# SiLU written back into its PSUM bank, and VectorE multiplying there, in a Strassen gate/up unit

## The chip, the cores and the metric

The kernel runs on one core of a Trainium2 chip. The metric is the device time of one execution in microseconds; the median of three runs of the kernel before is 1667.53 us. The engines are called as in the profile: PE (TensorE) does the matmuls and writes PSUM, ACT is ScalarE, DVE is VectorE, POOL is GpSimd, SP issues most of the DMAs.

## What is computed

One layer with two branches over a normalized input, sequence length 2048 and model width 576:

```python
xn = _layernorm(x, axis=-1)
s = _A_ref(xn, A_wqkv, A_w_phi, A_wo)        # linear attention, 32 heads of 18
g = _silu(_B_ref(xn, B_w_gate, B_w_up, B_w_down))
return x + s * g
```

The second branch is the one that matters here, a gated feed-forward network with a hidden width of 4608:

```python
def _B_ref(x, w_gate, w_up, w_down):
    g = _silu(x @ w_gate)
    u = x @ w_up
    return (g * u) @ w_down
```

Everything is float32. Matrix products run as three products of a rounded part and a remainder ("split"): a cast on ScalarE gives the rounded part, a subtraction on VectorE the remainder.

## The kernel before

The attention branch, the normalization and six of the 36 hidden tiles (128 hidden columns each, line 110, "early" tiles) come first and take about 541 us. The rest of the span is the feed-forward branch, and the change lies there.

The sequence is handled in two halves of 1024 rows (index i of the main loop, line 870). For each half, 30 hidden tiles are computed by `gate_up` (line 591), one call each, here called a unit; the six early tiles are fetched back from DRAM by `stored` (line 583). So there are 60 units in all. A unit forms the gate and the up product of 128 hidden columns with all 1024 rows. The gate and up weights beside each other and the two half blocks of rows make a 2x2 block product, which is done with seven block products in place of eight (Strassen's scheme with sums of blocks, Winograd's form). `product` (line 566) is one of them: seven matmuls of 512 columns into one PSUM bank.

A unit has four PSUM banks of 128x512 in view: x (`px`, two buffers, so that consecutive units alternate), y (`py`, one buffer) and w (`pw`, one buffer). The down part (`item`, line 785, and `tile_of`, line 685) has two buffers `pd` of two banks each. [...] In order of the program a unit does this:

- x gets product 0; ScalarE copies x to y (line 611); w gets product 4; y gets product 1 on top of the copy, and is then the gate product of the first row block;
- ScalarE applies SiLU to y and writes `h[0]`, an SBUF tile named `ha` (line 615);
- x goes on with products 5 and 2, and after each ScalarE copies it to an SBUF tile `s` (`snap`, line 596: s2 and s3);
- VectorE adds w to s3 (`add`, line 602; the add is line 604); x gets product 6 and is then the gate product of the second row block; SiLU writes `h[1]`, named `hb` (line 625), and VectorE multiplies it by s3 (line 626);
- w gets product 3, VectorE adds it to s2, and multiplies `h[0]` by s2 (line 630).

Between the products stand calls of `fill` (line 846). It emits matmuls of the down part from a queue: items that multiply finished h tiles, or sums of them, with rows of w_down, again by Strassen's scheme (`strassen`, line 730). The sums of h tiles and of w_down blocks are made on GpSimd (lines 753 to 779), then split (lines 58 and 59, the cast and the subtraction of `split`, used for h tiles `hh`, down weights `dw` and gate/up weights `w`). The result of an item is added to an accumulator in SBUF by VectorE (line 794; the accumulators are `acc`, `X` and `sx`). In the first half, the gate/up weights of the next tile are loaded and their sums made on GpSimd (lines 557 to 560) and split; they are also written to DRAM, and the second half reads them from there.

The program is written with a framework that tracks the tiles, sets the semaphores and lays out the instructions of each engine ahead of the run: each engine executes its queue in order, but that order is chosen by a planner from priorities (`tc.high_priority()`), the operands' modelled readiness and the buffers that are free. So it departs from the order of the program, as where the first product of the next unit runs ahead of the last product of this one. The last multiply of a unit is kept as an anchor (line 630): a few later groups of instructions are told to be issued behind it (`tc.issue_after`, lines 801 and 898).

Of the kernel before, what the change touches and what calls it, by code (L numbers as in the profile page):

```python
# [11 lines left out]
AF = mybir.ActivationFunctionType  # L12
# [34 lines left out]
def gated_hedgehog_kernel(ctx: ExitStack, tc, x, w_qk, w_v, w_phi, wo, w_gu, w_tail, w_down, ident_in, mask_in, out):  # L47
# [5 lines left out]
    nc = tc.nc  # L53
# [512 lines left out]
    def product(ps, w, m, b, first, last):  # L566
        mm = [(w[0][m][:, i], b[j]) for c in range(2) for i, j in ((c, c), (2 + c, c), (c, 3 + c))]
        mm += [(w[1][:, m], b[2][0:96])]
        for n, (l, r) in enumerate(mm):
            nc.tensor.matmul(ps, l, r, start=first and n == 0, stop=last and n == len(mm) - 1, skip_group_check=True)  # L570

    def short(name, bufs):
        return fq.tile([P, BT], F32, name=name, bufs=bufs)

    def h_tile():
        return [fp.tile([P, BT], F32, name=n, bufs=b) for n, b in (("ha", 7), ("hb", 6))]
# [6 lines left out]
    def stored(src, fill):  # L583
        h = h_tile()
        for r in range(2):
            nc.sync.dma_start(h[r], src[:, r * BT:(r + 1) * BT])
        for _ in range(4):
            fill()
        return h

    def gate_up(w, xo, fill, opening):
        A11, A12, A22, S2, S4, S3, S1 = xo
        xp, yp, wp = (fps.tile([P, BT], F32, name=n, bufs=b) for n, b in (("px", 2), ("py", 1), ("pw", 1)))
        h = h_tile()

        def snap(ps):
            t = short("s", 3)
            with tc.high_priority():
                nc.scalar.copy(t, ps)  # L599
            return t  # L600

        def add(ps, t):
            with tc.high_priority():
                nc.vector.tensor_add(t, ps, t)  # L604


        if opening:
            nc.tensor.matmul(yp, w[0][0][:, 0], A11[0], start=True, stop=True)
        product(xp, w, 0, A11, True, False)
        with tc.high_priority():  # L610
            nc.scalar.copy(yp, xp)  # L611
        product(wp, w, 4, S1, True, False)
        fill()
        product(yp, w, 1, A12, False, True)
        nc.scalar.activation(h[0], yp, AF.Silu)
        product(xp, w, 5, S2, False, False)
        s2 = snap(xp)
        fill()
        product(xp, w, 2, S3, False, False)
        s3 = snap(xp)  # L620
        add(wp, s3)
        fill()
        product(xp, w, 6, A22, False, True)
        with tc.high_priority():
            nc.scalar.activation(h[1], xp, AF.Silu)
        nc.vector.tensor_mul(h[1], h[1], s3)  # L626
        product(wp, w, 3, S4, False, True)
        add(wp, s2)
        with tc.high_priority():
            anchor.append(nc.vector.tensor_mul(h[0], h[0], s2))  # L630
        fill()
        return h

# [200 lines left out]
    queue, anchor, share = [], [], [2]  # L834
# [11 lines left out]
    def fill(lag=LAG):  # L846
        done = 0
        while queue and done < share[0] and (sum(c for q in queue for c, _ in q[2]) > lag or not queue[0][0]):
            look()
            c, item = queue[0][2].pop(0)  # L850
            item()
            done += c
            if not queue[0][2]:
                queue.pop(0)
# [15 lines left out]
    for i, n, f in units:  # L870
# [3 lines left out]
        if f >= EARLY:  # L874
# [3 lines left out]
            if todo and (i, f) != (0, NF - 1):  # L878
                ready.append(gate_up_weights(*todo.pop(0)))
        h = stored(h_dram[i, f], fill) if f < EARLY else gate_up(w, xo, fill, (i, f) == (0, EARLY))  # L880
        if n % 2 == 0:
            g = {"f": (f, units[units.index((i, n, f)) + 1][2]), "h": [h]}
# [58 lines left out]
```

## Time and profile before

| | |
|---|---|
| median of three runs | 1667.53 us (1667.0 to 1669.49) |
| span of the profiled execution | 1666.4 us |
| granted TensorE clock, mean | 0.997 |
| PE busy | 1621.8 us, 97% of the span |
| DVE busy | 1218.2 us, 73% |
| ACT busy | 718.3 us, 43% |
| POOL busy | 632.7 us, 38% |
| 60 units and the down part | from about 541 us to the end |

The profiled execution's time from first to last instruction is its span, 1.1 us below the median of the runs. PEld is TensorE's loading of weights, which overlaps the matmuls. In a row of groups or of the timeline stands the engine, the line of the kernel, the operation, the tile written and the tiles read (an arrow between them) and the shapes; a bracket at the end of a timeline row says how long the engine had been idle and whose result ended that. The waits view names the engine and line that waited, after the arrow the engine and line that it waited for, then the total in us, how many times, and the longest. The windows view gives, for a stretch of time, its length and the busy time and number of instructions of PE, PEld, DVE, ACT and POOL, then PE's granted clock, the DMA share and GB/s.

### The profile page before, as it was taken

What the parts mean: (1) busy time and instruction counts of PE and PEld (TensorE: products, weight loads), DVE (VectorE), ACT (ScalarE), POOL (GpSimd) and SP (SyncE); (2) the same over time, 40 slices, a digit from 0 to 9 for tenths busy, and PEclk for the clock granted to TensorE, in tenths of its full rate; (3) what the DMA queues carried; (4) which work ended last, traced back from release to release, by engine and by line L of the source; (5) the groups of instructions that cost most, each with busy time, mean ns of one, the idle gap of its engine ahead of it and who ended that gap; (6) DMA issues with size and microseconds to landing.
All of it is one profiled execution on the core that took longest, in us unless ns stands there. A gap on an engine that the chain in (4) does not pass through costs nothing.

```text
span 1666.4 us, 25130 instructions
## 1 busy us (share of the span) xinstructions
PE 1621.8 (97%) x9441; PEld 1437.4 (86%) x9441; DVE 1218.2 (73%) x1722; ACT 718.3 (43%) x1389; POOL 632.7 (38%) x660
## 2 busy tenths in 40 slices
PE   6999999999999999999999999999999999999998
PEld 5899998999987778888888888888888888888887
DVE  7678759899842577888788788836667667667678
ACT  5533345444431455454544544445433333433334
POOL 3466500433101453554455464413234234133132
PEclk9999999999999999999999999999999999999999
DMA  8623313334227636445544544495444555555534
GB/s 285 211 77 112 105 40 105 112 121 118 63 82 273 214 134 205 155 164 171 195 156 169 189 165 160 156 336 165 147 140 136 165 182 186 170 178 183 144 114 170
DMA packets 118108, 264.68 MB, mean 159 GB/s; under 512 B 12419, under 2 KB 48387, under 8 KB 116195
## 3 DMA queue, kind: packets, MB, share of 16 engines
q1 hardware_dynamic: 107628, 247.44, 45.1%
q0 software_dynamic: 3072, 11.02, 2.4%
q10 hardware_dynamic: 7286, 4.63, 0.9%
q8 instruction: 74, 1.21, 0.3%
q14 instruction: 48, 0.39, 0.1%
HBM read 164.21 MB, written 98.83 MB: 158 GB/s over the span
## 4 chain that ended last, share of the span: by engine, by line
PE 54%; DVE 8%; issue 1%; DMA 1%; POOL 0%; ACT 0%; DVEq 0%; POOLq 0%; ACTq 0%; SPq 0%
PE px L570 20%; PE pd L669 19%; PE pw L570 10%; PE py L570 5%; DVE hh L59 2%; DVE dw L59 1%; DVE ha L630 1%; DVE hb L626 1%; DVE acc L794 1%; DVE s L604 1%; DVE w L59 1%; DVE X L794 0%; DVE acc L641 0%; DMA ld<-in_B_w_gu 0%; POOL ld L560 0%
## 5 line engine op out<-in xcount | busy, mean ns | idle before, releaser
L669 PEld LDWEIGHTS pd<-dw,hh 128*128 128x128 f32 x3048 | 431.9, 189 | 41.1 <-DVE dw L59 7.2
L669 PE MATMUL pd<-dw,hh 128*128 128x288 f32 x3048 | 450.3, 298 | 15.8 <-DVE dw L59 5.9
L570 PE MATMUL px<-X,w 128*128 128x512 f32 x1440 | 375.2, 395 | 0.3 <-ACT s L599 0.3
L570 PEld LDWEIGHTS px<-X,w 128*128 128x128 f32 x1440 | 262.5, 189 | 53.1 <-ACT s L599 5.2
L570 PE MATMUL pw<-X,w 128*128 128x512 f32 x720 | 188.0, 397 | 1.8 <-DVE s L604 1.8
L570 PEld LDWEIGHTS pw<-X,w 128*128 128x128 f32 x720 | 133.4, 189 | 35.6 <-DVE s L604 6.7
L604 DVE TENSOR_TENSOR s<-pw,s 128x512 f32<-128x512 f32 x120 | 82.7, 689 | 105.3 <-ACT s L599 94.2
L92 PE MATMUL pe<-X,wh 128*128 128x512 f32 (+1 forms) x480 | 152.1, 400 | 1.6 <-POOL X L199 0.6
L794 DVE TENSOR_TENSOR acc<-pd,acc 128x576 f32<-128x576 f32 x128 | 96.0, 752 | 63.9 <-PE pd L669 63.4
L599 ACT COPY s<-px 128x512 f32<-128x512 f32 x120 | 70.3, 585 | 156.0 <-PE px L570 156.0
L58 ACT CAST hh<-ha 128x512 fp32r<-128x512 f32 x140 | 83.1, 619 | 107.3 <-PE pd L669 72.2
L59 DVE TENSOR_TENSOR hh<-ha,hh 128x512 fp32r<-128x512 f32 x140 | 114.1, 840 | 18.1 <-ACT hh L58 17.6
L92 PE MATMUL p<-KVWH,X 128*128 128x288 f32 (+1 forms) x640 | 123.7, 298 | 1.2 <-DVE phi L274 1.2
L92 PEld LDWEIGHTS pe<-X,wh 128*128 128x128 f32 (+1 forms) x480 | 88.6, 189 | 19.5 <-DVE h L120 1.4
L766 POOL TENSOR_TENSOR hb<-hb 128x512 f32<-128x512 f32 x34 | 46.3, 1360 | 154.8 <-DVE hb L626 154.4
L92 PEld LDWEIGHTS p<-KVWH,X 128*128 128x128 f32 (+1 forms) x640 | 100.6, 189 | 1.9 <-issue 1.6
L59 DVE TENSOR_TENSOR w<-ld,w 128x512 fp32r<-128x512 f32 (+1 forms) x90 | 73.5, 817 | 32.8 <-ACT w L58 32.8
L570 PE MATMUL px<-X,wt 96*128 96x512 f32 x240 | 95.0, 396 | 0.0
L570 PE MATMUL py<-X,w 128*128 128x512 f32 x360 | 93.8, 394 | 0.7 <-ACT py L611 0.7
L779 POOL TENSOR_TENSOR ha<-ha 128x512 f32<-128x512 f32 x34 | 52.3, 1552 | 104.5 <-DVE hh L59 104.5
L58 ACT CAST w<-ld 128x512 fp32r<-128x512 f32 (+1 forms) x90 | 49.4, 549 | 96.9 <-POOL ld L560 61.8
L753 POOL TENSOR_TENSOR h<-ha,hb 128x512 f32<-128x512 f32 x34 | 46.7, 1373 | 116.9 <-DVE ha L630 99.9
(181 smaller groups left out, 3105.6 us busy)
## 6 DMA issues: line engine op xcount, KB each, us to landing
w_dram<-w SPq DMA_DIRECT2D x87, 512.0 KB, 3.0
w<-w_dram SPq DMA_DIRECT2D x87, 512.0 KB, 4.7
wt<-t_dram SPq DMA_DIRECT2D x59, 336.0 KB, 4.7
ld<-in_B_w_gu SPq DMA_DIRECT2D x30, 512.0 KB, 4.6
X<-sum_dram SPq DMA_DIRECT2D x8, 1280.0 KB, 6.7
rt<-in_B_w_down SPq DMA_DIRECT2D x33, 288.0 KB, 3.2
rb<-in_B_w_down SPq DMA_DIRECT2D x33, 288.0 KB, 3.0
w_dram<-w SPq DMA_DIRECT2D x29, 256.0 KB
```

The costliest lines, as they stand in the source:

```text
L58: nc.scalar.copy(hi, src)
L59: nc.vector.tensor_sub(lo, src, hi)
L92: nc.tensor.matmul(ps, l, r, start=n == 0, stop=n == len(pairs) - 1)
L570: nc.tensor.matmul(ps, l, r, start=first and n == 0, stop=last and n == len(mm) - 1, skip_group_check=True)
L599: nc.scalar.copy(t, ps)
L604: nc.vector.tensor_add(t, ps, t)
L626: nc.vector.tensor_mul(h[1], h[1], s3)
L669: nc.tensor.matmul(ps, l, r, start=first and n == 0 and m == 0, stop=n == len(hs) - 1 and m == 2, skip_group_check=True)
L753: sub(s, g["h"][0][0], g["h"][0][1])
L766: nc.gpsimd.tensor_add(a21, a21, g["h"][1][1])
L779: sub(a12, a12, g["h"][0][0])
L794: nc.vector.tensor_add(a2, pd[:, :, 0:HALF], a2)
```

## The change

SiLU of y and of x no longer writes an SBUF tile: it overwrites its own PSUM bank. The two multiplies on VectorE read the bank as first operand and write the SBUF tile, which they overwrote in place before. The tiles `ha` and `hb` are so written for the first time by the multiplies.

```diff
         product(yp, w, 1, A12, False, True)
-        nc.scalar.activation(h[0], yp, AF.Silu)
+        nc.scalar.activation(yp, yp, AF.Silu)
         product(xp, w, 5, S2, False, False)
...
         with tc.high_priority():
-            nc.scalar.activation(h[1], xp, AF.Silu)
-        nc.vector.tensor_mul(h[1], h[1], s3)
+            nc.scalar.activation(xp, xp, AF.Silu)
+        nc.vector.tensor_mul(h[1], xp, s3)
         product(wp, w, 3, S4, False, True)
         add(wp, s2)
         with tc.high_priority():
-            anchor.append(nc.vector.tensor_mul(h[0], h[0], s2))
+            anchor.append(nc.vector.tensor_mul(h[0], yp, s2))
         fill()
         return h
```

## The prediction

> **What bounds the kernel now.** I read the busy shares first, then one stretch that holds the gate/up and down part alone, then the waits of TensorE in that stretch, then the two multiplies that the change rewrites, and last the timeline around the waits.
>
> ```profile
> PE 1621.8 (97%) x9441; PEld 1437.4 (86%) x9441; DVE 1218.2 (73%) x1722; ACT 718.3 (43%) x1389; POOL 632.7 (38%) x660
> ```
>
> ```profile
> 541.00:1660.00 1119.00, 1100.44 (x5983) 960.37 (x5982) 817.80 (x1103) 493.77 (x962) 447.46 (x388) 1.00 0.53 172
> ```
>
> TensorE bounds it. In the 1119 us in which the gate/up units run, PE is busy for 1100.4 us at a granted clock of 1.00; no matmul is added or removed, so the change can win at most the 18.6 us of idle PE, and it wins only where VectorE ends that idle time. The next view says who ends it.
>
> ```profile
> engine line waited for: us in total, times, longest us
> PE pd L669 <- DVE dw L59: 5.9, 4, 2.3
> PE pd L669 <- DVE sx L794: 4.1, 4, 1.0
> PE pd L669 <- DVE X L794: 3.5, 6, 1.0
> PE pw L570 <- DVE s L604: 1.8, 3, 0.6
> PE pd L669 <- ACT pd L690: 1.0, 2, 0.7
> PE py L570 <- ACT py L611: 0.7, 2, 0.3
> ```
>
> VectorE ends 15.3 of these microseconds. The four waits on dw fall before 612 us, where both multiplies nearly always take 0.69 us; I leave them out. For the rest the question is how late VectorE is because of the two multiplies.
>
> **What the change makes of the two multiplies.** Both still run on VectorE over 128x512, with the same sum tile from SBUF as second operand and the same output in SBUF; the first operand moves from SBUF to PSUM.
>
> ```profile
> L626 DVE TENSOR_TENSOR hb<-hb,s x60: 678/693/1647, 552.8 to 1643.5; 128x512 f32<-128x512 f32 x60
> L630 DVE TENSOR_TENSOR ha<-ha,s x60: 683/693/1812, 554.9 to 1645.7; 128x512 f32<-128x512 f32 x60
> L604 DVE TENSOR_TENSOR s<-pw,s x120: 672/692/693, 550.2 to 1644.5; 128x512 f32<-128x512 f32 x120
> L794 DVE TENSOR_TENSOR acc<-pd,acc x128: 741/752/760, 654.8 to 1646.3; 128x576 f32<-128x576 f32 x128
> ```
>
> (The three figures are shortest, median and longest, in ns.) With both operands in SBUF the multiply takes 693 ns at best and up to 1812. With one operand in PSUM, 120 adds of the same size never take over 693 ns, and 128 adds of 576 never over 760, though GpSimd works beside many of them. On the page's groups the means are 797 ns for L626 and 1118 for L630. At 692 ns each, 60 x (105 + 426) ns = 31.9 us of VectorE's busy time go. Most of that is slack; the timeline shows where it is not.
>
> [...]
>
> **Term A, the down accumulators behind L630.**
>
> ```profile
> 1198.07 1.61 POOL L771 TENSOR_TENSOR ha<-hb,ha 128x512 f32<-128x512 f32 x1
> 1198.47 1.77 DVE L630 TENSOR_TENSOR ha<-ha,s 128x512 f32<-128x512 f32 x1
> ...
> 1200.16 1.41 DVE L794 TENSOR_TENSOR sx<-pd,sx 128x576 f32<-128x576 f32 x2
> ...
> 1201.05 4.99 PE L669 MATMUL pd<-dw,hh 128*128 128x288 f32 x36 [1.02 <-DVE sx L794]
> ```
>
> GpSimd's subtraction runs until 1199.68; L630, started beside it, ends 0.56 us after that: the multiply stood still. The add that empties a down bank is next in VectorE's queue, and PE waits 1.02 us for it. At 0.69 us the multiply ends at 1199.16, the add (PSUM, not stretched) at 1199.9, 1 us before it ends now. The waits show four such places, 4.1 us. I take all: **-4.1**.
>
> **Term B, the up bank behind L626.**
>
> ```profile
> 1281.08 1.29 DVE L626 TENSOR_TENSOR hb<-hb,s 128x512 f32<-128x512 f32 x1
> ...
> 1283.28 0.68 DVE L604 TENSOR_TENSOR s<-pw,s 128x512 f32<-128x512 f32 x1
> ...
> 1284.01 1.63 PE L570 MATMUL pw<-X,w 128*128 128x512 f32 x6 [0.55 <-DVE s L604]
> ```
>
> L626 loses 0.60 us, L604 comes that much earlier, and the wait (three places, 1.8 us in all) goes but for some 0.1: **-1.7**.
>
> **Term C, L630 with another SBUF operation behind it.**
>
> ```profile
> 1056.30 1.61 POOL L771 TENSOR_TENSOR ha<-hb,ha 128x512 f32<-128x512 f32 x1
> ...
> 1056.69 1.77 DVE L630 TENSOR_TENSOR ha<-ha,s 128x512 f32<-128x512 f32 x1
> ...
> 1058.39 0.68 DVE L59 TENSOR_TENSOR w<-ld,w 128x512 fp32r<-128x512 f32 x1
> 1058.97 0.39 PE L570 MATMUL py<-X,w 128*128 128x512 f32 x1
> ...
> 1059.59 0.74 DVE L794 TENSOR_TENSOR X<-pd,X 128x576 f32<-128x576 f32 x1
> ...
> 1060.39 1.06 PE L669 MATMUL pd<-dw,hh 128*128 128x288 f32 x6 [1.03 <-DVE X L794]
> ```
>
> Here the split of L59, two SBUF operands, takes over the place beside GpSimd: the multiply would end at 1057.38, but L771 runs to 1057.91, so the split gains only about half of the 1.08 us. Of the wait of 1.03 I take 0.5, and 0.4 for a like one near 1616; the other four waits on X come behind no stretched multiply and stay: **-0.9**. For the nine short waits of the up bank in the weight loads and the two of 0.33 us on L611 (quoted below, behind a stretched L630 too) I put **-1.0**, between 0 and 2.2.
>
> **What it adds: the y bank is held longer.** Today y is free for the next unit's copy (L611) once SiLU (L615) has read it. Now it is held until L630 has multiplied, at the unit's end, and L611, the next unit's y and x products behind it and whatever stands behind L611 in ScalarE's queue wait for L630. L611 is issued early today, so it will wait nearly everywhere. What counts is when PE first uses y.
>
> ```profile
> 550.33 0.57 ACT L611 COPY py<-px 128x512 f32<-128x512 f32 x1 [0.18 <-PE px L570]
> ...
> 553.53 1.09 PE L570 MATMUL py<-X,w 128*128 128x512 f32 x4
> 553.73 0.32 SPq L555 DMA_DIRECT2D wt<-t_dram  x1
> 553.73 0.69 DVE L604 TENSOR_TENSOR s<-pw,s 128x512 f32<-128x512 f32 x1 [0.28 <-PE pw L570]
> 554.34 0.68 DVE L59 TENSOR_TENSOR w<-ld,w 128x512 fp32r<-128x512 f32 x1
> 554.48 1.66 PE L570 MATMUL pw<-X,w 128*128 128x512 f32 x6
> 554.94 0.68 DVE L630 TENSOR_TENSOR ha<-ha,s 128x512 f32<-128x512 f32 x1
> ```
>
> This is the first boundary between two units. PE fills the wait for L604 with four y matmuls, which the new wait forbids: L630 ends at 555.62, the copy takes 0.57, y is ready at about 556.25. The up product (554.48) covers the rest up to 556.2, and four matmuls of 0.23 us are left over: 0.95 us. The second boundary, at 565.5, has the same picture, and no down work is queued yet in either: **+2.0** together, from 0 (if the later wait of up to 2.3 us for dw swallows it) to 5.4 (if the order stays and y, at 553.53, waits until 556.25 both times). At the other 57 boundaries PE has down items and the up product ahead of y. Term C's rows show the tightest: y at 1058.97, L630 ending at 1058.46 today, at 1057.38 then, the copy done by 1058.0, 1 us to spare. They cost nothing; without that cover each would cost up to the 0.6 us of the copy.
>
> **What else moves.** SiLU writes PSUM in place; the nearest row is the copy between banks:
>
> ```profile
> L611 ACT COPY py<-px x60: 570/570/592, 541.6 to 1633.0; 128x512 f32<-128x512 f32 x60
> L599 ACT COPY s<-px x120: 577/587/592, 547.0 to 1640.3; 128x512 f32<-128x512 f32 x120
> ```
>
> So writing PSUM is 17 ns cheaper than SBUF, 2 us over 120 SiLUs on an engine that is busy 43%: 0. The x bank is held 0.7 us longer, until L626, but there are two of them and the next unit takes the other: 0. The h tiles are claimed by VectorE, later than by SiLU; that frees SBUF and adds a wait that SiLU had: 0. No DMA moves.
>
> The sum: -4.1 - 1.7 - 0.9 - 1.0 + 2.0 = -5.7 us on a span of 1666.4, so 1660.7. The median of the runs, 1667.53, lies 1.1 us above this span; on it I forecast **1661.8 us**.
>
> **The rivals.** *Slower: L611 slips behind a cast that waits for GpSimd.* The order on each engine is laid out ahead of the run by a planner that sees when operands are ready, and L611 is ready later now. Two units show today what happens when a weight cast goes first:
>
> ```profile
> 915.23 0.41 ACT L58 CAST w<-ld 128x256 fp32r<-128x256 f32 x1 [5.70 <-POOL ld L560]
> 915.54 0.58 ACT L611 COPY py<-px 128x512 f32<-128x512 f32 x1
> ...
> 916.17 1.21 PE L570 MATMUL py<-X,w 128*128 128x512 f32 x4 [0.33 <-ACT py L611]
> ```
>
> PE lost 0.33 us, and 0.5 against its own beat of 0.23 us a matmul. Weight casts exist in the first 29 units. If all flip at 0.5 us, the loss is 14.5 us and the time 1676; from 12 flips on it outweighs the 5.7 us, and 18 flips, which I take for this case, give 1661.8 + 9 = 1671. Against it: that cast hangs on a VectorE split that mostly stands behind L630 itself, so L611 should be ready first, and it has priority.
>
> *No change: the stretch moves on.* If VectorE's freed time only lets the next split of L59 collide with GpSimd, as in term C, also where another order sets in, half of A to C is left: -3.9 + 2.0, 1665.6 us. For it: L59's splits have both operands in SBUF and follow everywhere. Against it: at A's four places the next is an add from PSUM.
>
> *More.* The boundaries cost nothing, and the 0.6 us of waits on acc behind term A go too, with the full 2.2 us of small waits: 1667.5 - 9.5 = 1658.
>
> *The multiply isn't freed*, because something other than GpSimd stretches it: then +2.0, 1669.5. Against it: the adds of L604 and L794.
>
> **How the numbers follow.** My forecast 0.47, more 0.11, no change 0.20, slower by L611's place or another order 0.18, not freed 0.04. A time within 3.3 us (0.2%) of the median can't be told from no change. The forecast's own band, 1658.5 to 1664.5, leaves a little in that zone: faster 0.57, same 0.22, slower 0.21. The range, 1655 to 1671, takes in terms A to C with nothing given back below, the 5.4 us of the boundaries and those 18 flips above.
>
> **What would show it.** In the changed profile L626 and L630 should have a longest of about 0.70 us, and VectorE be busy some 30 us less; the four waits on sx and the three on s should be gone; L611's idle time should be ended by VectorE (L630); two short waits of y on L611 should stand between 550 and 570. Waits of y or x on L611 anywhere else, or an L611 behind a cast waiting on L560, would show the slower rival; splits of L59 that grew longer, the one of no change. If the order of the down items is quite different in the two traces, the sum is off whatever its terms.

## The result and the profile after

The changed kernel takes 1654.66 us (median of five runs, 1654.6 to 1655.92) against 1667.0 us (five runs, 1664.61 to 1669.49): a ratio of 0.9931, with a 95% interval of 0.9921 to 0.9942. (The ratio is taken over the single runs; the two medians alone would give 0.9926. Gains over the kernel before are such ratios taken of 1667 us.) That is 11.5 us of 1667, twice the 5.7 us of the forecast's sum. On the median that the forecast started from, 1667.53 us, this ratio is 1656.0 us, at the low end of the range, under the forecast's own band and under the 1658 us of the case "more".

The busy shares of the changed kernel, and the row of its windows view for the stretch of the gate/up units:

```profile
PE 1614.8 (98%) x9441; PEld 1434.1 (87%) x9441; DVE 1175.4 (71%) x1722; ACT 715.7 (43%) x1389; POOL 622.1 (38%) x660
```

```profile
541.00:1646.00 1105.00, 1094.63 (x5982) 958.78 (x5981) 774.76 (x1103) 491.32 (x962) 435.59 (x388) 1.00 0.53 174
```

VectorE is busy 42.8 us less (32.5 of it in the two multiplies, 9.5 in the splits of L59), GpSimd 10.6 us less. TensorE's idle time in the stretch falls from 18.6 us to 10.4. The profiled span, 1652.9 us, is 13.5 us shorter than the one before. So more than 5 us of it left time in which PE was shown as busy, and the 18.6 us of idle time, which the prediction took for the most that could be won, are not a bound.

The rows of the rewritten instructions (shortest, median and longest in ns) and those of one GpSimd sum, L560, first after and then before:

```profile
L615 ACT ACTIVATE py<-py x60: 562/582/589, 545.8 to 1622.7; 128x512 f32<-128x512 f32 x60
...
L626 DVE TENSOR_TENSOR hb<-px,s x60: 677/691/693, 553.5 to 1630.1; 128x512 f32<-128x512 f32 x60
...
L630 DVE TENSOR_TENSOR ha<-py,s x60: 677/684/693, 555.6 to 1632.3; 128x512 f32<-128x512 f32 x60
...
L560 POOL TENSOR_TENSOR ld<-ld,ts x30: 733/742/1186, 501.3 to 1056.4; 128x256 f32<-128x256 f32 x30
```

```profile
L560 POOL TENSOR_TENSOR ld<-ld,ts x30: 737/1056/1236, 500.6 to 1059.2; 128x256 f32<-128x256 f32 x30
```

No multiply is stretched any more: the longest is 693 ns, where it was 1647 and 1812. The last two rows show what the prediction did not look for. GpSimd's sum stood still beside VectorE's multiply just as the multiply did beside GpSimd; its median falls from 1056 to 742 ns, though nothing in it was edited.

Which of the two stands still depends on which starts second, as the 120 multiplies of the trace before show. In 41 of them a sum of GpSimd was already running when the multiply started; 36 of these took more than 0.9 us, and each of the 34 that took more than 1 us ended 0.55 us after that sum. The other 79 never took over 694 ns. In 16 of the 79 GpSimd started L560 while the multiply ran, and there L560 took 1.05 to 1.06 us.

The waits of PE in the same stretch:

```profile
PE pd L669 <- DVE dw L59: 4.8, 4, 1.5
PE pd L669 <- DVE X L794: 2.4, 5, 0.5
PE px L570 <- ACT w L58: 1.0, 2, 0.5
PE px L570 <- ACT s L599: 0.8, 2, 0.5
PE pd L669 <- ACT pd L690: 0.7, 1, 0.7
PE pd L669 <- ACT acc L640: 0.6, 1, 0.6
```

The four waits on sx and the three on s are gone, and the two of PE on L611 too. The first of the sx places, in the timeline:

```profile
1192.95 8.31 PE L669 MATMUL pd<-dw,hh 128*128 128x288 f32 x60
...
1194.36 1.62 POOL L771 TENSOR_TENSOR ha<-hb,ha 128x512 f32<-128x512 f32 x1
1194.75 0.68 DVE L630 TENSOR_TENSOR ha<-py,s 128x512 f32<-128x512 f32 x1
1195.35 0.74 DVE L794 TENSOR_TENSOR sx<-pd,sx 128x576 f32<-128x576 f32 x1
```

The multiply now runs through beside L771, the add follows at once, and PE does 60 down matmuls in a row where it had stopped after 24.

To see where the 13.5 us come from, take one event that each unit has, the start of SiLU on x (L625), and compare it unit by unit. The units are counted from 0; the last column is the move since the row above:

```
unit   before    after   after-before   step
  0     552.1    552.9      +0.74              ahead of the first boundary
  1     564.1    566.6      +2.50      +1.76   first boundary
  3     599.0    600.6      +1.58      -0.92
 18     889.8    889.7      -0.13      -1.71   five steps of -0.34
 24     994.2    992.3      -1.90      -1.77   two steps of -0.9
 35    1195.2   1191.5      -3.70      -1.80   X at 28; unit 30: -1.22, 31: +0.69
 46    1414.5   1402.9     -11.63      -7.93   sx at 36, 39, 42, 45; s at 40, 43
 53    1533.4   1521.5     -11.91      -0.28
 59    1642.9   1629.5     -13.43      -1.52   s at 54, X at 58
```

It is a staircase: a loss at the first boundary is there, 1.76 us where the forecast had 0.95, small steps repay it through the first half, and the large ones stand where the four waits on sx and the three on s stood.

### The profile page after: what moved, and what is told of

It is laid out like the page before. It is cut to its first block, busy times and chain, and to the rows that moved or that the text cites. A ratio compares the mean times of both kernels' runs of the same rounds, so it can differ in the third digit from the quotient of the medians.

```text
span 1652.9 us, 25205 instructions
## 1 busy us (share of the span) xinstructions
PE 1614.8 (98%) x9441; PEld 1434.1 (87%) x9441; DVE 1175.4 (71%) x1722; ACT 715.7 (43%) x1389; POOL 622.1 (38%) x660
## 4 chain that ended last, share of the span: by engine, by line
PE 64%; DVE 3%; DMA 1%; issue 1%; POOL 0%; ACT 0%; SPq 0%; DVEq 0%; POOLq 0%
PE px L570 23%; PE pd L669 22%; PE pw L570 11%; PE py L570 6%; PE pe L92 2%; DVE hh L59 1%; DMA ha<-h_dram 1%; DVE acc L641 0%; DVE dw L59 0%; DVE acc L794 0%; DMA X<-s_dram 0%; DMA rb<-in_B_w_down 0%; DVE w L59 0%; DVE X L794 0%; DVE ha L630 0%
## 5 line engine op out<-in xcount | busy, mean ns | idle before, releaser
L59 DVE TENSOR_TENSOR hh<-ha,hh 128x512 fp32r<-128x512 f32 x140 | 110.6, 815 | 23.6 <-ACT hh L58 23.0
L58 ACT CAST hh<-ha 128x512 fp32r<-128x512 f32 x140 | 83.1, 620 | 97.2 <-PE pd L669 79.9
L59 DVE TENSOR_TENSOR w<-ld,w 128x512 fp32r<-128x512 f32 (+1 forms) x90 | 76.3, 848 | 34.2 <-ACT w L58 33.2
L58 ACT CAST w<-ld 128x512 fp32r<-128x512 f32 (+1 forms) x90 | 49.4, 549 | 83.5 <-POOL ld L560 50.8
```

Source lines behind the costliest of these rows:

```text
L58: nc.scalar.copy(hi, src)
L59: nc.vector.tensor_sub(lo, src, hi)
```

## The experiments

The port theory, which the prediction argued: the gain is the time for which the two multiplies stood still beside GpSimd, because both their operands were in SBUF. ("Port" is a name only: no trace shows one.) The rival, called the order theory: the gain comes with the new order that the planner makes, and with the longer hold of the banks.

**The y side alone.** The first and the last edit of the diff; x as before.

> Only the y side is changed (SiLU in place in y, L630 from PSUM); L625 and L626 as before. Port theory (the gain is the time for which the multiplies stood still beside GpSimd, where it was on TensorE's path): L630 longest about 0.70 us, L626 still up to 1.65; the four waits on sx and the short ones on acc go, the three waits of the up bank on L604 (0.7 to 0.8 us each by TensorE's beat) stay; 7.5 to 9.5 us faster than before, so 2 to 4 us slower than the whole change. Order theory (the gain is the new order and the longer hold of the bank): about the whole 11.5 us, since the y bank is the one that is held.

Measured: 1658.61 us, ratio 0.9952 (0.9939 to 0.9964), 8.0 us faster. The rows of its two multiplies, and of its waits of PE that on the up bank:

```profile
L626 DVE TENSOR_TENSOR hb<-hb,s x60: 678/692/1296, 552.1 to 1635.2; 128x512 f32<-128x512 f32 x60
```

```profile
L630 DVE TENSOR_TENSOR ha<-py,s x60: 675/684/693, 554.3 to 1637.4; 128x512 f32<-128x512 f32 x60
```

```profile
PE pw L570 <- DVE s L604: 1.7, 3, 0.6
```

**The x side alone.** The middle edit of the diff (SiLU of x and L626).

> Only the x side is changed (SiLU in place in x, L626 from PSUM). Port theory: L626 longest about 0.70, L630 still up to 1.8; the three waits of the up bank go, the four on sx stay, no waits of x or y on L611 at the first boundaries; 2.5 to 4.5 us faster. Order theory: no change, within 1 us, since no bank that anything waits for is held longer.

Measured: 1663.7 us, ratio 0.9984 (0.9976 to 0.9993), 2.7 us faster. Its two multiplies:

```profile
L626 DVE TENSOR_TENSOR hb<-px,s x60: 677/691/693, 553.0 to 1638.6; 128x512 f32<-128x512 f32 x60
```

```profile
L630 DVE TENSOR_TENSOR ha<-ha,s x60: 681/693/1780, 555.2 to 1640.8; 128x512 f32<-128x512 f32 x60
```

Of its waits of PE, the three on s are gone and these stay:

```profile
PE pd L669 <- DVE sx L794: 4.1, 4, 1.0
PE pd L669 <- DVE X L794: 3.6, 6, 1.0
```

Each half takes away the waits that stand behind its own multiply and leaves the other's. The two gains, 8.0 and 2.7 us, add up to 10.7 of 11.5, within the intervals the whole. The order can be read from the traces, too: from 541 us on, VectorE, ScalarE and GpSimd each run their instructions in the same order with the x side alone as in the kernel before, so its 2.7 us owe nothing to a new order. In the whole change fewer than ten instructions each of VectorE and GpSimd stand elsewhere, on ScalarE some 15 of 963, mostly weight casts and L611 that changed places, and of PE's 5982 matmuls some 50, nearly all before 590 us.

**The hold without the operand.** Does holding y make a better order?

```diff
             anchor.append(nc.vector.tensor_mul(h[0], h[0], s2))
+            nc.vector.tensor_copy(s2[:, 0:1], yp[:, 0:1])
```

> The kernel before, with one more VectorE copy of one column from y behind L630, so that y is held as long as in the change while both multiplies still read SBUF. Port theory: L630 and L626 as long as before, none of the gain; 2 us slower for the first two boundaries, plus up to 3 for L611 behind stretched multiplies and the 60 small copies: 1 to 5 us slower than before. Order theory: most of the 11.5 us appears without any operand in PSUM.

Measured: 1673.04 us, ratio 1.0042 (1.0028 to 1.0055): 7 us slower, more than either theory expected. Its row of the y side's multiply, those for the added copy with what waited for it, and PE's wait on L611 (the down part is a line further on):

```profile
L630 DVE TENSOR_TENSOR ha<-ha,s x60: 681/693/1818, 553.7 to 1650.5; 128x512 f32<-128x512 f32 x60
```

```profile
L631 DVE COPY s<-py x60: 141/148/163, 554.4 to 1651.8; 128x1 f32<-128x1 f32 x60
...
  ACT py L611: 85.0, 22
```

```profile
PE py L570 <- ACT py L611: 4.3, 7, 1.0
PE pd L670 <- DVE s L631: 4.1, 4, 1.0
```

**The control**, the same copy without the hold:

```diff
             anchor.append(nc.vector.tensor_mul(h[0], h[0], s2))
+            nc.vector.tensor_copy(s2[:, 0:1], h[0][:, 0:1])
```

> The control for the kernel that only holds y: the same small copy behind L630, 60 times, but reading h[0] in SBUF, so that y is free early as before. Theory that the hold itself cost most of the 7 us there: this one within 2 us of before. Theory that VectorE's 60 copies and their semaphores cost it: 4 to 7 us slower than before.

Measured: 1666.11 us, ratio 1.0002 (0.9993 to 1.0011). So the copies cost nothing that can be measured, and the 7 us are the hold. The rival is refuted: the hold alone loses. It also fits that the hold is cheap in the change because the multiply that ends it is short. With a stretched multiply in front of it, L611 comes late for PE seven times; in the change, with 0.69 us, PE's own view has no wait on L611, and its weight loads have two, of 0.5 us, at the first two boundaries.

**The other operand in PSUM.** The sum stays in the w bank and SiLU writes SBUF; y is not held.

```diff
-        add(wp, s2)
         with tc.high_priority():
-            anchor.append(nc.vector.tensor_mul(h[0], h[0], s2))
+            nc.vector.tensor_add(wp, wp, s2)
+            anchor.append(nc.vector.tensor_mul(h[0], wp, h[0]))
```

> The kernel before, but the last add of a unit overwrites the w bank, and L630 multiplies h[0] (SBUF, SiLU as before) by w in PSUM: the other operand comes from PSUM, y is not held. Port theory: what matters is that one operand is in PSUM, whichever it is, so L630's longest falls to about 0.70 us and the four waits on sx go, a gain of 7 to 8 us as with the y side alone; against it w is held 0.7 us longer, until L630, and the next unit's up product waits that long where no down item covers it, 0 to 12 us. So between 8 us faster and 4 us slower, with L630 short. If what matters is SiLU writing PSUM or y being held: L630 as long as before.

Measured: 1666.52 us, ratio 1.0004 (0.9994 to 1.0013). The row of its multiply, and the largest of its waits of PE:

```profile
L630 DVE TENSOR_TENSOR ha<-pw,ha x60: 677/684/693, 555.1 to 1644.0; 128x512 f32<-128x512 f32 x60
```

```profile
PE pw L570 <- DVE ha L630: 7.4, 11, 1.4
```

The multiply is freed just as well, its longest 693 ns with either operand in PSUM. Two of the four waits on sx go and two of 0.5 us are left. But the up product needs w at once, and 11 new waits eat the gain. The bank has to be one that is not wanted soon.

**GpSimd's neighbours left out.** In the kernel before and in the changed one, the three sums that work in place on h tiles (lines 766, 771 and 779) are dropped, so the down products run on unsummed tiles.

> The kernel before without three of GpSimd's sums of h tiles (the ones that work in place on h, lines 766, 771 and 779 there); the down products then run on unsummed tiles. These sums lie beside some 24 of the 32 us for which L626 and L630 are stretched. Port theory: L630's mean falls from 1.12 us to 0.70 to 0.85, the waits on sx go, 7 to 12 us faster than before. Otherwise: L630 stays stretched, under 3 us faster.

> The changed kernel with the same three sums left out. Port theory: with the neighbours gone the operand's place matters little more, so the difference to the kernel of before without these sums shrinks from 11.5 us to 2 to 5 (what L626 loses beside the sums of w_down, which stay). If the gain comes from the order or the hold: still about 11 us between the two.

Measured: 1652.83 us (0.9916, 0.9902 to 0.9930) for the kernel before without them, 1647.25 us (0.9883, 0.9867 to 0.9899) for the changed one without them. The first is 14 us faster than the kernel before, more than the 7 to 12 expected. Other waits shrink with the sums as well (PE's on X go, those on dw fall from 5.9 to 3.0 us), so this time alone does not show what the neighbours cost the multiply; its length does. The groups view of the former, with mean ns after the busy time:

```profile
L626 DVE TENSOR_TENSOR hb<-hb,s 128x512 f32<-128x512 f32 x60 | 47.9, 798 | 48.6 <-ACT hb L625 47.0
...
L630 DVE TENSOR_TENSOR ha<-ha,s 128x512 f32<-128x512 f32 x60 | 43.1, 719 | 0.7
```

With its neighbours gone L630's mean falls from 1118 to 719 ns with no edit of its own, while L626, which runs beside sums of w_down that stay, keeps its 798. The change is then worth 5.6 us in place of 11.5. That is a little above the 2 to 5 expected, by less than the intervals can tell apart; the trace still has the five short steps of the first half, behind L560, 1.7 us in all.

So much the traces show of the stall: with one operand in PSUM the longest multiply goes from 1812 to 693 ns and the median of L560 from 1056 to 742 ns, and on both sides it was the instruction that started second that lost time (34 multiplies of over 1 us behind a running sum, L560 16 times at 1.05 to 1.06 us behind a running multiply and at 0.74 in the change), while L771, which started first, keeps its length (1.61 us in term A's rows, 1.62 in the change). Why the second one stands still, no trace shows.

**The two first boundaries.** The y side of units 0 and 1 stays as before.

```diff
-        nc.scalar.activation(yp, yp, AF.Silu)
+        gate = yp if held else h[0]
+        nc.scalar.activation(gate, yp, AF.Silu)
...
-            anchor.append(nc.vector.tensor_mul(h[0], yp, s2))
+            anchor.append(nc.vector.tensor_mul(h[0], gate, s2))
```

> The whole change, but in the first two units the y side stays as before (SiLU into ha, multiply in SBUF), so that y is free early at the two boundaries where no down work is queued. Port theory: the step of 1.8 us at the second unit and part of the 0.7 at the first go, all else as in the change: 1.5 to 2.5 us faster than the change, about 0.992 of before. If the boundaries cost nothing because the later waits for dw swallow them: the same as the change.

Measured: 1654.35 us, ratio 0.9928 (0.9915 to 0.9940), the same as the change. The waits at the boundaries go and with them the step at unit 1, but the waits on dw behind them grow from 4.8 to 5.6 us, and TensorE's granted clock drops after the longest of them (0.58 from 573.0 to 575.5 us, an estimated 1.5 us by the late matmul starts; more on such drops below), which it does not in the change. The lower bound of the prediction's term, 0, was the right one.

**Two further edits on top of the change.** The same edit at the end of the second half (lines 640 and 641):

> The change, and the same edit in the last step of the second half (lines 640 and 641: SiLU in place in the down bank, the multiply reads it from PSUM). Port theory: the nine multiplies of line 641, up to 2 us today, fall to 0.75, but they stand near the end behind the last down products, where only the last two or three are on the path, and the down bank is held 0.75 us longer: between 1 us faster and 1 us slower than the change.

Measured: 1655.54 us, ratio 0.9938 (0.9925 to 0.9952), no better than the change. Its row of the multiply, and two of its waits of PE:

```profile
L641 DVE TENSOR_TENSOR acc<-pd,X x9: 457/758/759, 1634.3 to 1649.8; 128x576 f32<-128x576 f32 x7, 128x288 f32<-128x288 f32 x2
```

```profile
PE pd L669 <- ACT pd L690: 3.4, 6, 1.3
...
PE pd L669 <- DVE acc L641: 1.0, 1, 1.0
```

The longest multiply falls from 1993 to 759 ns, but the time does not: PE's waits on L690 grow from 0.7 to 3.4 us, and one on the multiply itself comes.

The order behind the anchor at line 801, taken away:

```diff
-                with tc.issue_after(anchor[-1].ins) if first and i == 0 else ExitStack():
+                with ExitStack():
```

> The change without the order that puts the first down preparations of the first half behind the last multiply (line 801). It asks what the waits on dw before 613 us (4.8 us in the changed kernel, the largest that are left) hang on. If on that order: they shrink, 1 to 4 us faster than the change. If on VectorE's splits beside GpSimd: the same as the change within 1 us, or slower, as the splits of the gate/up weights then come later.

Measured: 1651.59 us, ratio 0.9908 (0.9894 to 0.9922), 3 us faster than the change. The waits on dw vanish; a new one comes, of which its waits of PE show

```profile
PE px L570 <- ACT s L599: 3.1, 2, 2.7
```

Together with the old form in the first two units:

> The two edits together: no order behind the anchor for the first down preparations, and the y side of the first two units as before. If the first boundaries cost what TensorE's beat shows (1.8 us) and only the later waits for dw swallowed the saving: 1 to 2.5 us faster than without the anchor alone, about 0.990 of before. If they are swallowed by something else (the wait on the copy s at 552 us): no faster than without the anchor.

Measured: 1651.57 us, 0.9907 (0.9892 to 0.9922), no faster. Here no wait on dw is left to swallow a saving, so those waits are not the whole account of the boundaries. In the traces the step at unit 1 falls from 1.71 to 0.55 us, and 0.7 us of that are left at the last unit, too little for these runs to show. Where the rest goes stays open. Alone on the kernel before:

> The kernel before without the order behind the anchor. If that order and the change act on different waits: 2 to 4 us faster than before (0.998), as on top of the change. If its gain needs the change: no faster than before.

Measured: 1663.98 us, 0.9981 (0.9973 to 0.9990), 3.2 us faster. So this edit and the change act on different waits and add up; the changed kernel without that order, with or without the old form in the first two units, is the fastest version with the full computation that was run.

## Why the prediction was right, and where its sizes were off

The direction and the mechanism were right: the multiplies are freed, the gain sits behind them, and each half of the edit does its own part. The sum was half of what was measured. The range held it, but in part by luck: its lower end, 1655 us, is not worked out from the terms, since A to C with nothing given back come to 1667.5 - 6.7 = 1660.8 us, and the median of the changed kernel's runs as it stands, 1654.66 us, lies just under it. Point by point, with the steps of the table of units, which count everything that TensorE loses and not just the idle time that the view shows:

- *Term A* (-4.1): the steps at units 36, 39, 42 and 45 are -1.09, -1.11, -1.73 and -1.67, so -5.6. About 1.1 each is the wait on sx; at two of them the wait on acc that follows went too, which the prediction had kept for its "more" case.
- *Term B* (-1.7): the steps at units 40, 43 and 54 are -0.82, -0.87 and -0.93, so -2.6. This is a size: the idle time shown for each was 0.55 to 0.64 us, but TensorE lost 0.7 to 0.8 to the wait (the distance of two matmul starts less their beat of 0.23 us) and some 0.1 more on the matmul after it. The prediction used that beat for the cost of the slower rival and the shown idle time for the gains.
- *Term C* (-0.9): units 28 and 58 give -0.57 and -0.58, so -1.2. About right.
- *The short waits* (-1.0): this term failed most. The steps of -0.34 (five in the first half), of -0.9 at units 20 and 24 and of -0.3 at units 34, 37, 46 and 50 come to -4.8. Two things were wrong. The six steps of the second kind and the third, 3.1 us, stand where the term's own short waits of the up bank and of L611 stood; it was mis-sized, above even its upper bound of 2.2. (Three of the four -0.3 steps come with the y side alone as well as with the x side alone, and two even with the small copy of the control, so they do not all hang on the change itself.) And the five steps, 1.7 us, were left out: GpSimd is freed too. L560 ends 0.3 us earlier beside L630, and the weight cast, the split and the add of a down bank behind it come earlier with it; ahead of four of the five steps PE ran a row of 48 down matmuls in 6.8 us with no wait in its own view, and in the change in 6.55. The five steps are there with the y side alone and with the sum in PSUM, and absent with the x side alone.
- *The boundaries* (+2.0): the loss is real, +1.76 at unit 1, but units 2 and 3 give back 0.9, and without the loss the time is the same: the lower bound. It did not come as forecast: the two waits of y on L611 that PE was to show are not there. The planner put matmuls into x in their place, and PE waits on a weight cast (0.48 and 0.52 us, the row of L58 above) and on the copy s. Part of what units 2 and 3 give back is that the kernel before loses time there to a drop of the clock to 0.50, about 1.4 us by the late matmul starts, which the change does not (last section). L611 stands behind the cast of the slower rival:

```profile
556.63 0.41 ACT L58 CAST w<-ld 128x256 fp32r<-128x256 f32 x1 [1.82 <-POOL ld L560]
556.95 0.58 ACT L611 COPY py<-px 128x512 f32<-128x512 f32 x1
```

- *The other 57 boundaries* (0): right, but only together with the short multiply. The hold alone costs 7 us. L611's idle time ends with L630 13 times, not nearly everywhere.
- *SiLU into PSUM* (0): 14 ns less each (582 ns, 596 before), as the copies said.
- *The slower rival*: its order did come. L611 starts directly behind a weight cast that waited for L560 in 11 units, in 2 before, so the prediction's argument that L611 would be ready first was wrong. Its price did not come: PE shows no wait on L611 in any of them and has other work, except at the first two boundaries. *No change*: its sign shows in one place, the splits of the weights, 848 ns on average against 817 before, 2.8 us in all; those of ha take 815 against 840, and L59 as a whole runs 9.5 us less, so the stretch was not taken over.
- *Readings*: the 693 ns called the multiply's best are its median; the shortest are 678 and 683, which changes nothing in the sum. With the first operand in PSUM the medians are 684 ns (L630) and 691 (L626).

## What to carry to other kernels

When VectorE and GpSimd work side by side, look at the longest of a VectorE operation and not its median: here a longest of over twice the median with both operands in SBUF (1812 and 693 ns) was VectorE time that came back when one operand was read from PSUM (longest 693), and GpSimd's L560, which had started second 16 times, got shorter (median 1056 to 742 ns). It is a gain only as far as something on the path waits behind it (L641 went from 1993 to 759 ns for nothing). The price is the bank, held until the multiply is done; take one whose next writer has other work ahead of it (y here, not w, which brought 7.4 us of waits on L630, and not the down bank, where those on L690 grew from 0.7 to 3.4 us). When a gain is summed from waits of a busy TensorE, take the distance of matmul starts less their usual beat (0.7 to 0.8 us for a wait in term B), not the idle time in the row (0.55 to 0.64).

## What the runs showed of the hardware that was not expected

TensorE's granted clock fell to half for a few microseconds after some of the waits for dw near 572 us, and not after others of the same length. The windows view of two microseconds behind that wait (PE's granted clock is the third figure from the end), in the kernel before after a wait of 2.35 us, with the y side alone after 1.54, in the changed kernel after 1.53, and with the hold alone after 2.19:

```profile
572.60:574.60 2.00, 2.00 (x6) 1.61 (x6) 2.00 (x4) 0.00 (x0) 1.54 (x2) 0.50 0.47 190
```

```profile
573.40:575.40 2.00, 2.00 (x8) 1.81 (x8) 2.00 (x5) 0.00 (x0) 0.93 (x1) 0.50 0.00 0
```

```profile
574.40:576.40 2.00, 2.00 (x14) 1.67 (x13) 2.00 (x6) 0.18 (x1) 0.56 (x1) 1.00 0.00 0
```

```profile
573.60:575.60 2.00, 2.00 (x14) 1.69 (x13) 2.00 (x6) 0.16 (x1) 0.56 (x1) 1.00 0.00 0
```

At half clock a matmul of 512 columns starts every 0.43 us in the kernel before where it is 0.23 otherwise, and one of 288 columns every 0.24 us with the y side alone where it is 0.13. In the kernel before five starts come about 0.2 us late and three more 0.1 to 0.16, so this drop costs about 1.4 us and is part of the 13.5 us between the two spans. What decides whether it comes was not tried.
